# Sparse attention into a gated MLP: a new start-up, k copied out of PSUM, and a plan that prices tile-mode changes

## The chip, the cores and the metric

The kernel runs on one core of a Trainium2 chip. A core has TensorE (PE: matmuls; weight loads are listed apart as PEld), VectorE (DVE), ScalarE (ACT), GpSimd (POOL), a queue engine (SP), and DMA engines that move data between HBM and the on-chip memory SBUF. Matmuls write into a small second memory, PSUM. The metric is the time of one execution on the device in microseconds (us), the median of three runs.

## The reference, cut to what matters

```python
# q, k, v: (4, 8, 768, 64) float32; chunks of 32 keys, 24 chunks, top_k = 6
k_min, k_max = k_chunks.min(axis=3), k_chunks.max(axis=3)
ub = sum(maximum(q * k_min, q * k_max), axis=-1)      # bound of a query for a chunk
ub = where(causal, ub, -1e9)
top_chunks = argsort(ub)[..., -6:]
mask = chunk_is_selected & (pos_q >= pos_k)
attn = softmax(where(mask, q @ k.T / 8, -1e9)) @ v
x = attn, heads side by side                          # (3072, 512)
h = x @ w_in                                          # (512, 2048)
out = (h * clip(h + 3, 0, 6) / 6) @ w_out             # (2048, 512)
```

The first 192 queries have at most six chunks behind them, so the selection matters for the other 576 only.

## The kernel before

**Attention.** Two heads of one batch form a pair; there are 16 pairs, four per batch. A pair passes through these steps, named by the letters of the plan:

- k, q, v: loads of 384 KB each, as two DMA issues, one per head. The first pair's second halves of k and q go out on ScalarE's queue, everything else on SP's.
- K: six fp32 transposes on PE (tile KT, in PSUM); DVE reduces each 32 keys to maximum (KM) and minimum (KC) and subtracts; ScalarE casts KT to bf16 (LHS). All three read KT in PSUM.
- Q: six transposes (QT); ScalarE copies them to SBUF (QTS); DVE clips at zero (QP); GpSimd casts QTS to bf16 (RHS).
- U: 24 small matmuls, 64 rows by 32 columns of the array, give the chunk bounds (UBP); DVE adds the causal bias (UBT).
- V: four transposes (UBQ); twelve 8-maximum searches on DVE; a comparison with the sixth largest gives SEL.
- L: three transposes (SLT) and a copy (SELT).
- S: scores in six groups per pair (tile SPS, matmuls with 64 rows, two heads side by side in the array). To each group further matmuls of EM with SELT add a large negative number at chunks that were not selected. ScalarE takes the exponential (PT); GpSimd zeroes what lies above the diagonal.
- C: GpSimd casts v to bf16 (VB), with a column of ones.
- P: 21 matmuls per head (PVP); DVE divides by the sum and writes to the row block Xb.

**MLP.** Tokens go in eight groups of 384, two per batch. X transposes Xb (XTP), H multiplies by w_in (tile HP, 64 blocks of eight matmuls), ScalarE and DVE form the gated value GT, and O multiplies by w_out (tile OP, 24 output tiles, each of four blocks of four matmuls). ScalarE scales each output tile and SP stores it. The weights come in eight chunks (w0 to w3 for w_in, w4 to w7 for w_out), issued from GpSimd's queue and cast to bf16 on the way.

**What sets the order.** Nothing is looped in program order. All operations go into a list scheduler (class Plan) that knows a duration for each, their dependencies and the number of buffers per ring (for instance three large PSUM buffers, "big", shared by KT, QT, UBP, SPS and HP). For each engine it takes the operation that could start first; PE may choose, among those that could start within 0.1 us of each other, the one that stands earlier in a long written list of tokens (SEQUENCE). The instructions are then emitted in that order, so every engine works strictly through its own list and waits in place. Weight chunks are tied to the cast of a certain pair's v by WGATE.

On PE the operations use three tilings of the array: U uses 64 by 32, S uses 64 by 128, and the others a single tile.

Lines of the profile: KT and QT transposes L301, reductions L311, subtraction L319, LHS L326, QTS L337, QP L341, RHS L347, UBP L360, UBT L368, UBQ L382, SLT L410, SPS L440 and L445, exponential L451, diagonal L455, PVP L480, HP L537, OP L561, output copy L567, store L570. Constants are made once, ahead of the first operation (L230 to L253).

Of the kernel before, what the change touches and what calls it, by code (L numbers as in the profile page):

```python
# [15 lines left out]
P = 128  # L16
CH = 32
# [5 lines left out]
LAT = {"PE": 0.22, "DVE": 0.09, "ACT": 0.09, "POOL": 0.09, "LD": 2.0, "ST": 2.0}  # L23

# [6 lines left out]
class Op:  # L31
    def __init__(self, eng, dur, tok, key, fn, deps, take, use):
        self.eng, self.dur, self.tok, self.key, self.fn = eng, dur, tok, key, fn
        self.deps = [d for d in deps if d is not None]
        self.take = take
        self.end = None
        for t in list(take) + list(use):
            t.users.append(self)
        self.banks = [t for t in list(take) + list(use) if t.ring in ("big", "sm")]


class Plan:


    def __init__(self, rings, start, place):
        self.place = place
        self.rings = {r: [None] * n for r, n in rings.items()}
        self.count = {r: 0 for r in rings}
        self.free = dict(start)
        self.ops = []  # L50
        self.last = {}

    def add(self, eng, dur, tok, fn=None, deps=(), take=(), use=(), chain=None):
        deps = list(deps)
        if chain is not None:
            deps.append(self.last.get(chain))
        op = Op(eng, dur, tok, self.place(tok), fn, deps, take, use)
        if chain is not None:
            self.last[chain] = op
        self.ops.append(op)  # L60
        return op
# [18 lines left out]
    def run(self, slack):  # L80
# [9 lines left out]
        while any(cand.values()):  # L90
            best = None
            for eng, lst in cand.items():
                mine = None
                for op in lst:
# [3 lines left out]
                    at = max(r, self.free[eng])  # L98
                    s = slack.get(eng, 0.0)
# [9 lines left out]
            self.free[op.eng] = op.end  # L109
            for b in op.take:  # L110
                b.slot = self.count[b.ring] % len(self.rings[b.ring])
                self.rings[b.ring][b.slot] = b
                self.count[b.ring] += 1
# [8 lines left out]

SEQUENCE = """
V0 S0.2 R0 K0 k2 q1 R3 w7 q0 S0.4 S0.1 U0 k3 v5 v0 R1 P0.0 v6 w4 S3.0 R2 S0.0 v1 S0.3 S0.5 V2 V4 k0 w0 k4 w6 Q3
V3 K1 L2 q5 P0.1 v3 w5 S2.2 R7 k1 Q1 R6 k5 H1.8 O1.2.8 w3 K2 H1.6 S3.1 v10 L5 S3.5 L3 q3 S3.4 U2 K4 C5 K3 R4
S3.2 H1.10 v2 O1.2.4 S3.3 H1.4 Q8 X1.2 Q7 Q2 S1.3 P-1.0 K5 L0 P-1.1 R5 S2.5 w2 H2.0 S1.0 k7 S2.0 V11 S1.1 K6 V5
H1.2 q4 S11.1 O1.2.0 H0.10 H2.2 U1 q11 O3.2.8 C0 P2.0 H0.0 k6 R9 S1.5 S1.2 H2.4 H1.14 K8 H2.6 L7 S1.4 S4.4 H1.0
H0.8 U6 Q6 v8 k11 H2.12 V6 Q4 w1 H4.6 P1.0 k9 H2.10 S4.5 S2.1 L4 O1.1.12 S4.2 Q0 q8 S2.4 U3 v4 U9 H4.4 H0.6  # L130
H0.12 v11 O3.0.8 P7.0 S4.3 R10 S7.0 S2.3 P5.0 P3.0 S4.0 H4.12 U5 P4.1 O1.1.8 H2.14 S4.1 S5.4 P5.1 S5.1 H4.0 K10
P6.1 H1.12 U4 U8 X5.0 C4 L8 U7 k14 H4.2 R8 O1.2.12 q7 v7 H4.10 H0.2 Q5 v15 S5.3 q6 H6.10 S6.2 S5.0 X1.0 v9 H7.2
k12 H4.8 V7 C14 K9 O3.1.0 H0.4 C3 v12 O1.0.12 O1.1.4 S5.2 S5.5 S6.1 H2.8 P9.0 S6.3 S7.5 v13 S7.1 V10 H0.14 X6.0
q14 S6.5 P4.0 P6.0 H7.12 S6.4 R11 V1 V8 K7 O3.0.4 C2 k8 O1.1.0 X2.0 O3.2.0 C10 O3.2.12 S7.2 O1.0.0 v14 S10.2 C9
P1.1 P10.0 P11.0 O0.1.8 O1.0.4 P2.1 S6.0 P8.0 O0.2.8 Q9 L1 X7.2 U10 X0.0 P11.1 S9.0 H6.0 S9.4 L6 S7.4 S7.3 X4.0
H3.12 O3.0.0 P8.1 O3.1.8 q10 H7.4 q2 R15 S9.3 C1 P7.1 O0.2.4 V9 O0.1.12 H5.2 X0.2 P9.1 L12 O3.0.12 K11 H3.6 Q10
Q11 P3.1 H5.14 U13 S10.4 O1.0.8 H7.0 H6.12 S8.5 S8.0 O3.1.12 S8.2 O0.0.12 X5.2 O3.2.4 O0.0.4 S9.1 S10.1 S13.5
H6.4 U12 P10.1 O2.0.0 q9 V13 S13.1 L14 H6.6 S10.5 Q12 H6.14 L9 S8.3 C11 X3.2 P12.1 L11 H7.14 R12 O3.1.4 S8.4 C6
H4.14 P14.0 S9.2 S10.0 S10.3 X2.2 S12.2 U14 H5.4 X6.2 S11.4 S8.1 S13.0 X3.0 H3.8 P12.0 O0.1.0 U11 S9.5 S14.4 K12
S11.3 L10 O0.0.0 C12 R14 O4.0.8 O4.1.8 O2.0.8 k10 H3.10 O0.2.12 X7.0 C8 O4.0.0 k15 O2.0.4 H3.4 O4.1.0 S13.3 C13  # L140
L15 S13.2 O2.1.8 O2.1.4 H3.0 O2.0.12 C7 O0.1.4 V15 H7.6 K13 q13 H3.2 H6.8 O2.2.8 S11.2 S11.5 H5.10 O2.1.12 S14.1
K14 S12.4 S11.0 S14.0 O4.2.8 K16 H7.8 H5.8 q15 Q16 k13 H6.2 O4.2.0 H3.14 O0.0.8 H5.12 O4.2.12 K17 U15 S12.5
P13.1 O0.2.0 O4.1.12 Q15 K15 P14.1 Q17 O4.1.4 O4.0.4 U16 V16 O2.2.12 K18 O2.1.0 L16 Q14 Q18 S14.5 Q13 H7.10
S13.4 S12.1 q12 P15.1 U17 V17 H5.0 O4.2.4 K19 S12.0 S16.0 O2.2.4 S12.3 V12 L17 S15.1 S14.2 Q19 X4.2 S16.1 S16.2
U18 S16.3 L13 V18 S16.4 O2.2.0 V14 O5.1.0 S16.5 O4.0.12 H5.6 S15.3 C15 S14.3 P13.0 O5.0.0 S15.0 O5.2.12 P15.0
O6.0.12 O6.1.0 O5.2.4 O5.0.8 S15.2 S15.4 O5.1.4 O5.1.12 O7.0.8 O6.0.8 O6.0.0 O7.1.8 O5.2.8 O7.1.4 O6.0.4 S15.5
O6.2.12 O6.2.0 O6.2.4 O5.1.8 O7.0.12 O7.0.4 O6.2.8 R13 O7.2.0 O7.1.12 O6.1.4 O6.1.12 O6.1.8 O7.2.12 O7.2.4
O7.0.0 O7.2.8 O7.1.0 O5.2.0 O5.0.12 O5.0.4
# [4 lines left out]
def place(tok):  # L153
    return POS.get(tok, 0)
# [3 lines left out]
def kernel(  # L158
# [31 lines left out]
    rings = dict(big=3, sm=2, ks=3, qs=3, vb=3, vs=3, qts=3, qp=2, kc=4, lhs=4, rhs=4, ubt=2, sel=2, selt=3,  # L190
                 pt=9, x=4, xt=2, gt=2, u=3, ot=2)
    plan = Plan(rings, dict(PE=2.0, DVE=3.2, ACT=2.2, POOL=5.0, LD=0.3, ST=0.0), place)
# [23 lines left out]
    THREE = const.tile([P, 1], FP32, name="THREE")  # L216
    EM = const.tile([P, 2, S], BF16, name="EM")
# [13 lines left out]
    def constants():  # L231
        make_identity(nc, IDENT32[:])
        nc.vector.memset(THREE[:], 3.0)
        for t in fixed["kc"]:
            nc.vector.memset(t[:], 0.0)
# [16 lines left out]
        for g in range(4):  # L252
            nc.vector.tensor_copy(EM[g * CH:(g + 1) * CH, g % 2], E32[:])  # L253


    st = [dict() for _ in range(NP)]

    def plan_loads(i):
# [4 lines left out]
        def ld(buf, x, name):  # L263
            t = new(buf, [P, NBLK, 2, D], FP32, name)
            for e in range(2):
                (nc.scalar if i == 0 and e == 1 and x is not v else nc.sync).dma_start(
                    t[:, :, e, :], natural(x, b, 2 * hp + e))
# [4 lines left out]
        s["ldk"] = add("LD", 2.07, f"k{i}", lambda: ld(s["ks"], k, "KS"), take=[s["ks"]], chain="ldk")  # L272
        s["ldq"] = add("LD", 2.07, f"q{i}", lambda: ld(s["qs"], q, "QS"), take=[s["qs"]], chain="ldq")
        lv = add("LD", 2.07, f"v{i}", lambda: ld(s["vs"], v, "VS"), take=[s["vs"]], chain="ldv")
        s["o_v"] = add("POOL", 0.86, f"C{i}", castv, deps=[lv], take=[s["vb"]], use=[s["vs"]], chain="castv")

    WGATE = (2, 2, 3, 3, 4, 4, 5, 5)

    def plan_weights():
# [3 lines left out]
        for n in range(4):  # L283
# [4 lines left out]
            res.append(add("LD", 3.1, f"w{n}", None, deps=[iss], chain="w"))  # L288
        for n in range(4):
# [4 lines left out]
            res.append(add("LD", 3.1, f"w{n + 4}", None, deps=[iss], chain="w"))  # L294
# [8 lines left out]
    UDUR = 0.74  # L303

    def plan_K(i):
        s, tok = st[i], f"K{i}"
        kt = Buf("big")
        s["kc"], s["lhs"] = Buf("kc"), Buf("lhs")
        tr = add("PE", 0.66, tok, lambda: transposed(kt, s["ks"], "KT"), deps=[s["ldk"]], take=[kt], use=[s["ks"]], chain="K")
        def stat(op, dst):  # L310
            nc.vector.tensor_reduce(out=dst, in_=kt.obj[:, 0:S].rearrange("p (c w) -> p c w", w=CH), axis=AX.X, op=op)  # L311
# [5 lines left out]
        def sub():  # L317
            t = fx(s["kc"])
            nc.vector.tensor_tensor(out=t[:, 0, 0:NCH], in0=s["KM"][:], in1=t[:, 1, 0:NCH], op=A.subtract)  # L319
        a1 = add("DVE", 0.95, tok, smax, deps=[tr], use=[kt])  # L320
        a2 = add("DVE", 0.95, tok, lambda: stat(A.min, fx(s["kc"])[:, 1, 0:NCH]), deps=[tr, a1], take=[s["kc"]],
                 use=[kt], chain="kc")
        s["o_kc"] = add("DVE", 0.45, tok, sub, deps=[a2], use=[s["kc"]])

        def lhs():
            nc.scalar.copy(new(s["lhs"], [P, S], BF16, "LHS")[:], kt.obj[:, 0:S])  # L326
        s["o_lhs"] = add("ACT", 0.80, tok, lhs, deps=[a2] if i == 0 else [tr], take=[s["lhs"]], use=[kt], chain="lhs")

    def plan_Q(i):
# [13 lines left out]
        s["o_qp"] = add("DVE", 0.62, tok, part, deps=[up], take=[s["qp"]], use=[qts], chain="qp")  # L343
        s["qts"], s["o_qts"] = qts, up
# [5 lines left out]
    def plan_U(i):  # L350
# [13 lines left out]
        o = add("PE", UDUR, tok, mm, deps=[s["o_kc"], s["o_qp"], s["o_qts"]], take=[ub],  # L364
# [56 lines left out]
    def plan_S(i, m):  # L421
# [31 lines left out]
        def mask():  # L453
# [4 lines left out]
        o = add("PE", 0.09 + cols / 2400.0, tok, mm, deps=[s["o_lhs"], s["o_rhs"], s["o_slt"]], take=[sp],  # L458
                use=[s["lhs"], s["rhs"], s["selt"]])
        x = add("ACT", 1.03 if w > 256 else 0.40, tok, ex, deps=[o], take=[pt], use=[sp])  # L460
# [41 lines left out]
    def plan_mlp(g, wdma):  # L502
# [52 lines left out]
        def do_o(t, acc):  # L555
            ps, ot = Buf("sm"), Buf("ot")
# [15 lines left out]
            add("ST", 0.70, "", store, deps=[c], use=[ot], chain="store")  # L572

# [20 lines left out]
    small = ctx.enter_context(tc.tile_pool(name="small", bufs=4))  # L594
    for i in range(NP):
        plan_loads(i)
    wdma = plan_weights()
    for i in range(NP):
        for f in (plan_K, plan_Q, plan_U, plan_V, plan_L):
            f(i)  # L600
        for m in range(len(BINS)):
# [43 lines left out]
```

The softmax here doesn't subtract the row's maximum and nothing guards it: scores larger than these inputs give would overflow.

## Time and profile before

The median is 314.17 us (313.96 to 317.83 in three runs); the profiled execution spans 314.1 us.

| engine | busy us | share | instructions |
|---|---|---|---|
| PE | 292.0 | 93% | 2992 |
| PEld | 178.4 | 57% | 2992 |
| DVE | 173.8 | 55% | 464 |
| ACT | 178.6 | 57% | 217 |
| POOL | 78.1 | 25% | 149 |

| the program's parts on PE | matmuls | busy us |
|---|---|---|
| O (OP, L561) | 384 | 88.9 |
| H (HP, L537) | 512 | 85.9 |
| scores (SPS, L440 and L445) | 640 | 67.4 |
| k and q transposes (L301) | 192 | 29.8 |

Busy shares are means over stages with different limits: the first 60 us are attention alone, from then on attention of later pairs runs between the MLP's blocks, and the last 45 us are MLP alone. What counts for a change is therefore where in the span PE isn't busy, and at what clock it runs. A matmul's busy time can overlap the next one's, so the time of a block is better read from its start to the start of what follows it. DMA moves 29.82 MB, 24.78 MB of it through SP's and ScalarE's queue, most of it in the first third.

### The profile page before, as it was taken

To read this page: it belongs to the slowest core of one execution; us is meant where nothing else is said; L and a number is where in the kernel's file an instruction comes from. 1 tells how busy PE (TensorE), PEld (TensorE's weight loads), DVE (VectorE), ACT (ScalarE), POOL (GpSimd) and SP (SyncE) were. 2 spreads that over 40 slices of the span, in tenths; PEclk is the share of its full clock that TensorE was granted. 3 is DMA by queue.
4 is the path that set the end of the run, shared out by engine and by line. 5 is a ranking of instruction groups with operands and counts; after the bars stand their busy time and mean duration, and the time that the engine had idled before them with its cause. 6 is when DMAs were issued, how large, how long until landed. Compare 5 with 4: busy or idle time off the path is not lost.

```text
span 314.1 us, 7230 instructions
## 1 busy us (share of the span) xinstructions
PE 292.0 (93%) x2992; PEld 178.4 (57%) x2992; DVE 173.8 (55%) x464; ACT 178.6 (57%) x217; POOL 78.1 (25%) x149
## 2 busy tenths in 40 slices
PE   3569789889999999999999999999999999999995
PEld 2437557556665566466656566466646655665442
DVE  7358777757574854287656656157705612577100
ACT  0338878747857456176868554366464781566111
POOL 7137667411312032150343013130120221000000
PEclk9979999979999999999999999999999999999999
DMA  9994999996402575550232000100011000000121
GB/s 210 279 262 86 221 219 212 218 257 140 102 16 66 138 182 129 146 136 1 49 88 53 0 33 35 69 33 2 0 35 68 2 35 35 33 0 3 44 89 67
DMA packets 82976, 29.82 MB, mean 95 GB/s; under 512 B 75776, under 2 KB 79872, under 8 KB 82944
## 3 DMA queue, kind: packets, MB, share of 16 engines
q1 hardware_dynamic: 77152, 24.78, 32.1%
q0 software_dynamic: 4224, 4.19, 8.2%
q10 hardware_dynamic: 1568, 0.39, 0.6%
q8 instruction: 23, 0.38, 0.5%
q14 instruction: 9, 0.07, 0.1%
HBM read 27.26 MB, written 6.29 MB: 107 GB/s over the span
## 4 chain that ended last, share of the span: by engine, by line
PE 87%; DVE 5%; ACT 3%; DMA 2%; POOL 1%; issue 1%; SPq 0%; ACTq 0%; POOLq 0%
PE OP L561 27%; PE HP L537 26%; PE PVP L480 7%; PE SPS L440 7%; PE SPS L445 5%; PE UBP L360 4%; PE KT L301 3%; PE QT L301 3%; DMA QS<-in_q_dram 2%; PE UBQ L382 2%; PE XTP L517 2%; ACT PT L451 1%; DVE KM L311 1%; PE SLT L410 1%; DVE EM L253 1%
## 5 line engine op out<-in xcount | busy, mean ns | idle before, releaser
L451 ACT ACTIVATE PT<-SPS 128x1024 bf16<-128x1024 f32 (+1 forms) x96 | 83.1, 924 | 21.8 <-PE SPS L445 19.6
L561 PE MATMUL OP<-WOUT,GT 128*128 128x512 bf16 x384 | 88.9, 379 | 0.0
L537 PE MATMUL HP<-XT,WIN 128*128 128x384 bf16 x512 | 85.9, 326 | 0.0
L541 ACT ACTIVATE U<-HP,THREE 128x768 bf16<-128x768 f32 x64 | 57.7, 902 | 35.5 <-PE HP L537 35.5
L547 DVE SCALAR_TENSOR_TENSOR GT<-U,HP 128x768 bf16<-128x768 bf16 x64 | 61.0, 953 | 27.6 <-ACT U L541 27.6
L537 PEld LDWEIGHTS <-WIN 128*128 128x128 bf16 x512 | 49.5, 98 | 32.1 <-issue 0.7
L455 POOL TENSOR_SCALAR_AFFINE_SELECT PT<-PT 128x256 bf16<-128x256 bf16 x96 | 38.6, 408 | 111.5 <-ACT PT L451 111.2
L561 PEld LDWEIGHTS <-GT 128*128 128x128 bf16 x384 | 35.5, 98 | 40.6 <-issue 2.4
L567 ACT ACTIVATE OT<-OP 128x512 f32<-128x512 f32 x24 | 14.4, 600 | 51.6 <-PE OP L561 41.0
L440 PE MATMUL SPS<-RHS,LHS 64*128 64x512 bf16 (+3 forms) x256 | 35.0, 315 | 0.8 <-ACT PT L451 0.7
L445 PE MATMUL SPS<-SELT,EM 64*128 64x288 bf16 (+6 forms) x384 | 32.4, 252 | 0.0
L347 POOL CAST RHS<-QTS 128x768 bf16<-128x768 f32 x16 | 15.7, 984 | 40.7 <-ACT QTS L337 39.5
L480 PEld LDWEIGHTS <-PT 128*128 128x128 bf16 x672 | 23.4, 97 | 2.8 <-issue 1.0
L445 PEld LDWEIGHTS <-EM 64*128 64x128 bf16 x384 | 18.7, 96 | 7.9 <-issue 1.0
L311 DVE TENSOR_REDUCE KM<-KT 128x24 f32<-128x768 f32 x16 | 15.1, 956 | 11.9 <-PE KT L301 11.8
L440 PEld LDWEIGHTS <-LHS 64*128 64x128 bf16 x256 | 11.3, 95 | 14.0 <-issue 10.8
L301 PE MATMUL KT<-IDENT_111,KS 128*128 128x128 f32 x96 | 14.6, 296 | 4.6 <-DMA KS<-in_k_dram 4.2
L326 ACT CAST LHS<-KT 128x768 bf16<-128x768 f32 x16 | 12.8, 801 | 10.1 <-DVE KM L311 8.5
L490 DVE TENSOR_TENSOR Xb<-PVP,RINV 128x384 bf16<-128x384 f32 x32 | 17.7, 556 | 1.0
L301 PE MATMUL QT<-IDENT_111,QS 128*128 128x128 f32 x96 | 15.2, 304 | 2.6 <-DMA QS<-in_q_dram 2.2
L368 DVE TENSOR_TENSOR UBT<-UBP,BIAS 96x384 f32<-96x384 f32 x16 | 8.8, 551 | 15.1 <-PE UBP L360 15.0
L337 ACT COPY QTS<-QT 128x768 f32<-128x768 f32 x16 | 12.6, 804 | 5.6 <-PE QT L301 5.5
(103 smaller groups left out, 217.4 us busy)
## 6 DMA issues: line engine op xcount, KB each, us to landing
VS<-in_v_dram SPq DMA_DIRECT2D x32, 192.0 KB, 3.5
out_dram<-OT SPq DMA_DIRECT2D x24, 256.0 KB, 2.0
KS<-in_k_dram SPq DMA_DIRECT2D x31, 192.0 KB, 3.2
QS<-in_q_dram SPq DMA_DIRECT2D x31, 192.0 KB, 3.4
WIN<-in_moe_w_in_dram POOLq DMA_DIRECT2D x4, 512.0 KB, 9.2
WOUT<-in_moe_w_out_dram POOLq DMA_DIRECT2D x4, 512.0 KB, 8.4
KS<-in_k_dram ACTq DMA_DIRECT2D x1, 192.0 KB, 3.3
QS<-in_q_dram ACTq DMA_DIRECT2D x1, 192.0 KB, 4.3
```

Source lines behind the costliest of these rows:

```text
L301: nc.tensor.transpose(T[:, j * P:(j + 1) * P], src.obj[:, j].rearrange("p e d -> p (e d)"), IDENT32[:])
L311: nc.vector.tensor_reduce(out=dst, in_=kt.obj[:, 0:S].rearrange("p (c w) -> p c w", w=CH), axis=AX.X, op=op)
L440: nc.tensor.matmul(T[:, e, c:c + hi - lo], lhsT=s["lhs"].obj[e * D:(e + 1) * D, j * P:(j + 1) * P], rhs=s["rhs"].obj[e * D:(e + 1) * D, lo ...
L445: nc.tensor.matmul(T[:, e, c:c + hi - lo], lhsT=EM[e * D:(e + 1) * D, h, j * P:(j + 1) * P], rhs=s["selt"].obj[e * D:(e + 1) * D, x:x + hi ...
L451: nc.scalar.activation(T[:, :, 0:w], sp.obj[:, :, 0:w], ACT.Exp, scale=scale)
L455: nc.gpsimd.affine_select(out=dv, in_=dv, pattern=[[0, 2], [1, P]], compare_op=A.is_ge, fill=0.0, base=0, channel_multiplier=-1)
L480: nc.tensor.matmul(T[:, qb, :], lhsT=t[:, e, c:c + P], rhs=fx(s["vb"])[:, e, j, :], start=(j == 0), stop=(j == qb))
L490: nc.vector.tensor_tensor(out=xb[b].obj[:, :, h * D:(h + 1) * D], in0=pv.obj[:, :, 0:D], in1=s[("ri", e)][:].to_broadcast([P, NBLK, D]), o ...
L537: nc.tensor.matmul(T[:, f, 0:GRP], lhsT=WIN[:, kt, (f0 + f) * P:(f0 + f + 1) * P], rhs=xt.obj[:, kt, :], start=(kt == 0), stop=(kt == KT_H ...
L541: nc.scalar.activation(new(u, [P, 2, GRP], BF16, "U")[:], hp.obj[:, :, 0:GRP], ACT.Relu, bias=THREE[:], scale=1.0)
L547: nc.vector.scalar_tensor_tensor(out=gt.obj[:, f0:f0 + 2, :], in0=u.obj[:], scalar=6.0, in1=hp.obj[:, :, 0:GRP], op0=A.min, op1=A.mult)
L561: nc.tensor.matmul(T[:, :], lhsT=gt.obj[:, f, t * P:(t + 1) * P], rhs=WOUT[:, f, :], start=(f == 0), stop=(f == FT - 1))
```

## The change

It has five parts.

1. Start-up. A one-column exponential (WARM) right after the constant THREE makes ScalarE load its function table at once. Ten transposes of the identity ahead of the first k transposes, and nine behind the first q transposes, keep PE at work while it would wait (plan_warm); their results are not used. The four copies that fill EM move from DVE to GpSimd.
2. Loads. v is planned after the next pair's q, and the weights' gates change.
3. From pair 1 on, ScalarE copies the transposed k to SBUF as fp32 (KTS); the reductions and the cast to LHS, now on GpSimd, read that copy. Pair 0 stays as it was.
4. The plan counts a change of PE's tiling as 0.095 us (SWITCH) and asks that a pair's scores follow all of the pair before; some planned durations change, and SEQUENCE is a new list, so the order is new throughout.
5. The last output tile is computed, copied and stored in two halves of 256 columns (do_last).

```diff
-    def add(self, eng, dur, tok, fn=None, deps=(), take=(), use=(), chain=None):
+    def add(self, eng, dur, tok, fn=None, deps=(), take=(), use=(), chain=None, mode=0):
...
                     at = max(r, self.free[eng])
+                    if eng == "PE" and op.mode != self.mode:
+                        at += SWITCH
...
+        nc.scalar.activation(WARM[:], THREE[:], ACT.Exp, scale=-1.0)
...
         for g in range(4):
-            nc.vector.tensor_copy(EM[g * CH:(g + 1) * CH, g % 2], E32[:])
+            nc.gpsimd.tensor_copy(EM[g * CH:(g + 1) * CH, g % 2], E32[:])
...
+        s["ldv"] = add("LD", 2.07, f"v{i}", lambda: ld(i, s["vs"], v, "VS"), deps=[st[min(i + 1, NP - 1)]["ldq"]],
+                       take=[s["vs"]], chain="ldv")
...
-    WGATE = (2, 2, 3, 3, 4, 4, 5, 5)
+    WGATE = (0, 0, 0, 4, 4, 0, 8, 3)
...
+        direct = i == 0
+        if direct:
+            src, up = kt, tr
+        else:
+            def copy():
+                nc.scalar.copy(new(kts, [P, S], FP32, "KTS")[:], kt.obj[:, 0:S])
+            src, up = kts, add("ACT", 0.80, tok, copy, deps=[tr], take=[kts], use=[kt], chain="kts")
...
         def lhs():
-            nc.scalar.copy(new(s["lhs"], [P, S], BF16, "LHS")[:], kt.obj[:, 0:S])
+            (nc.scalar.copy if direct else nc.gpsimd.tensor_copy)(new(s["lhs"], [P, S], BF16, "LHS")[:], src.obj[:, 0:S])
...
-        o = add("PE", 0.09 + cols / 2400.0, tok, mm, deps=[s["o_lhs"], s["o_rhs"], s["o_slt"]], take=[sp],
+        o = add("PE", 0.02 + cols / 2400.0, tok, mm, mode=1, deps=[s["o_lhs"], s["o_rhs"], s["o_slt"]] + (st[i - 1]["S"] if i else []), take=[sp],
...
+    def plan_warm(n, after):
+        w = Buf("sm")
+
+        def mm():
+            T = new(w, [P, P], FP32, "WRM")
+            for _ in range(WARMUP[n]):
+                nc.tensor.transpose(T[:], IDENT32[:], IDENT32[:])
+        return add("PE", 0.2 * WARMUP[n], f"W{n}", mm, deps=[after], take=[w], chain="warm")
```

WARMUP is (10, 9). In do_last the only new operations are 32 matmuls of 128x256 in place of 16 of 128x512, and two copies and two stores of half the size.

## The prediction

> **What bounds the kernel now.** I read the slices first, then stage windows, then the timeline of the stages that are not full, and last the chain for prices. Slices of the page (each 7.85 us; tenths):
>
> ```profile
> PE   3569789889999999999999999999999999999995
> ...
> PEclk9979999979999999999999999999999999999999
> DMA  9994999996402575550232000100011000000121
> ```
>
> The reader should see that PE is full from about slice 9 to the last one, that the DMA engines are full in slices 0 to 8, and that the clock dips in slices 2 and 8. The stage windows (us; PE, PEld, DVE, ACT, POOL busy; clock; DMA share; GB/s):
>
> ```profile
> 4.15:22.00 17.85, 10.70 (x89) 7.53 (x91) 10.73 (x28) 4.39 (x5) 5.74 (x8) 0.94 1.24 280
> 22.00:60.40 38.40, 34.21 (x581) 25.04 (x578) 28.57 (x99) 32.23 (x39) 26.44 (x47) 0.99 1.05 187
> 60.40:67.30 6.90, 4.71 (x30) 3.16 (x28) 3.92 (x28) 1.70 (x2) 0.82 (x1) 0.77 1.14 252
> ...
> 80.00:310.60 230.60, 229.99 (x2171) 134.14 (x2167) 120.04 (x286) 129.77 (x161) 39.68 (x80) 1.00 0.20 57
> 310.60:314.10 3.50, 0.00 (x0) 0.00 (x0) 0.00 (x0) 0.59 (x1) 0.00 (x0) 0.88 0.20 75
> ```
>
> From 80 us on PE idles 0.6 of 230.6 us, so the end is PE's sum of work plus what PE lost before 67.3 us plus a 3.5 us tail. The timeline of the lossy stages:
>
> ```profile
> 4.15 1.51 PE L301 MATMUL KT<-IDENT_111,KS 128*128 128x128 f32 x6 [4.15 <-DMA KS<-in_k_dram]
> ...
> 8.12 1.28 ACT L326 ACT_TABLE_LOAD   x1 [8.12 <-DVE KC_122 L311]
> ...
> 17.66 1.04 DVE L341 TENSOR_SCALAR QP<-QTS 128x576 f32<-128x576 f32 x1
> ...
> 17.80 0.30 PE L410 MATMUL SLT<-IDENTB,SEL_126 96*128 96x96 bf16 x3 [1.43 <-DVE SEL_126 L393]
> ...
> 64.04 1.47 PE L301 MATMUL QT<-IDENT_111,QS 128*128 128x128 f32 x6 [2.19 <-DMA QS<-in_q_dram]
> ...
> 65.94 0.45 PE L410 MATMUL SLT<-IDENTB,SEL_127 96*128 96x96 bf16 x3
> ```
>
> Six transposes take 1.5 us cold against 0.66 later; a table load of 1.28 us stands in the first pair's chain; at 61.9 us PE waits 2.2 us for a q load and comes back cold. Prices from the chain of waits in order of time (start, us):
>
> ```profile
> 90.33 1.33 PE PVP L480 x42
> ...
> 99.31 1.97 PE KT L301 x18
> ...
> 104.73 0.80 PE UBP L360 x24
> ...
> 154.48 0.97 PE OP L561 x4
> ...
> 157.02 0.86 PE OP L561 x4
> ...
> 268.99 20.80 PE HP L537 x128
> 289.79 20.73 PE OP L561 x96
> ```
>
> Six k or q transposes are 0.655, a PVP head 0.67, an H group of eight 1.30, an O group of four 0.86; the same O group is 0.97 when a differently tiled matmul follows, so a change of tile mode costs 0.10. A UBP block ends in one such change, so it is 0.70 itself. From starts to starts in the full stretch also: UBQ 0.33, SLT 0.13, six XTP 0.34, the six score groups of a pair 2.27.
>
> **What the Trainium skill says.** (1) "TensorE: Matmul & The Clock Gate", Part 1: the clock is halved until one window of about 3.4 us has been busy, and falls back after an idle one. The trace agrees: its clock records are 3.41 us long, and the q transposes at 64.04 take 1.47 us. (2) The same page, Part 4, says that the clock doesn't engage for transposes. The trace disagrees: the SLT at 17.80 ran in 0.30 us, the warm length (0.45 at 65.94, cold), and the window before it (12.9 to 16.3) held mostly k, q and UBQ transposes. So transposes as clock keepers can work. A window 57% busy (2.7 to 6.1) did not warm the clock, however. (3) "TensorEngine Tiling (Array Packing)", Key Properties: changing the tiling mode drains TensorE; the 0.10 us above is that. (4) "GPSIMD Engine Reference", Specifications: its SBUF interface is shared with VectorE in two-port modes; QP took 1.04 us at 17.66 beside an RHS cast, 0.46 alone at 10.95.
>
> **The change, part by part.**
>
> Constants. The first ACTIVATE sits behind the loads instead of at 8.12, so the 1.28 us table load leaves the chain. The four EM copies (0.58 each) go from DVE to GpSimd: KM of pair 0 starts at 5.7, not 6.21. EM is needed only by the first score mask, after 15 us, so four GpSimd copies of 0.6 to 0.8 us, from 6.0 to about 9, cost nothing. The price: the second q half is issued on ScalarE's queue behind the table load, and may be issued 1.3 us later (issue at 1.33 before). Then q lands near 7 instead of 5.65. Hidden if the clock is warm, because the LHS copy of pair 0 precedes QTS on ScalarE and ends near 8.45 anyway.
>
> First chain: KT 4.15 to 5.66, KM and KC 5.7 to 7.6, LHS 7.6 to 8.45, QTS to 9.25, QP to 9.75, UBP at 9.8 (11.46 before). The warming transposes (10 from about 1.5 us at 0.25 cold, 9 after QT) make PE nearly continuous from 1.5 us on, so the clock should be full by then: UBP 0.80 instead of 1.52, ending 10.6 instead of 12.98. They lie in time when PE waits for loads. If the clock stays cold, the 9 (2.3 us) and the k transposes behind them (1.5 us) stand in front of UBP and it starts near 12.
>
> Then DVE in its new order: UBT 0.55, two reductions of pair 1 1.9, maxima 1.16, QP 0.46 to 1.04, subtraction 0.2 to 0.8, selection 0.45, two reductions of pair 2 1.9, SELT 0.3: 6.9 to 8.1, taken as 7.4. Mask matmuls follow, and the first exponential starts near 18.7 (22.0 before; 21.5 if cold).
>
> k copied to SBUF: ScalarE's 0.80 us copy replaces its 0.80 us cast, so ScalarE pays nothing; GpSimd gets 15 casts of 0.83 to 1.12 us (about 15 us), beside 78 busy of 314. In the attention stage this makes it 6 x 0.41 + 3 x 1.0 = 5.5 us a pair against ScalarE's 7.2: not the bound, though masks and DMA issues queue behind casts. The KT bank comes free after one 0.8 us copy, not after two reductions and a cast (2.7 us), which feeds the score groups better.
>
> Loads. v moves behind the next pair's q. Weight chunks, in before all eight issued between 26 and 54 us, stand in the built GpSimd order three after the first v cast (about 16 us), three after 26 score masks (about 51), two after 42 (about 73). Queue 0 took 8.2% of the span for eight, 3.2 us of all engines each. The jam of 30 to 64 us goes, and with it the 2.2 us wait for q and the cold stretch behind it: from 60.4 to 67.3 PE did 3.05 us of warm work, so 3.85 us come back. The last two chunks took 8.4 us to land before; needed near 89, they land by 85.
>
> Order of PE. Counting the built orders: mode changes 134 before, 116 after. Ahead of the first H group, before has 7 k and 7 q blocks, 7 UBP, 6 UBQ, 5 SLT, 29 score groups, 8 PVP, 2 XTP: 33.65 us, and 38 changes. After has 7, 7, 7, 7, 7, 38, 10, 4: 39.8 us, and 44 changes. So 6.15 us of work move ahead of the first H, and behind it 24 fewer changes (72 for 96) give 2.3 us.
>
> When does the first H start? Between the first exponential and H, ScalarE has 38 exponentials (32 of 1.03, 6 of 0.40) and 8 copies of 0.80: 41.9 us; PE has 38 us there. ScalarE becomes the bound of this stage. It was 94% busy in the densest ten microseconds before (50 to 60), 84% over 22 to 60.4. I take 94%: 18.7 + 44.6 = 63.3, less 2 us by which PE runs ahead through the three PSUM buffers: H at 61.3 (60.4 before).
>
> Tail. The last O tile is in two halves: the final copy is about 0.40 (the 128x256 exponential) for 0.60, the store half as large: 0.4 us.
>
> Sum: 314.1 + 0.9 - 6.15 - 2.3 - 3.85 - 0.4 = 302.3.
>
> **Rivals.** (A) As above, 302, chance 0.62; it needs ScalarE at 90% or more. (B) Better: a warm head and ScalarE at 100%, H at 58.6: 299.6, less 2 if the first exponential comes at 17: 298. For it: buffers and loads run well ahead. Against: ScalarE and PE are both near full and any slip shows. 0.18. (C) The new wait takes back most of it: the head stays cold (exponential at 21.5) and ScalarE stays at 84%: H at 21.5 + 49.9 - 2 = 69.4, end 310.4. For it: the late q half breaks PE's busy stretch, and a 57% window didn't warm. 0.15. (D) Slower: on top of C, GpSimd holds masks or the last weight chunks behind its casts, and O waits one landing of 8.4 us and returns cold (1.7): 320. Against: 16 us of slack, GpSimd at 75%. 0.05.
>
> **Numbers.** A is the likeliest: 302. B reaches down to 297; A and half of C reach up to 308.5, which leaves about 2 in 10 outside. 2% faster is 307.9: A, B and a little of C, 0.84; slower by 2% is part of D, 0.03; the rest 0.13.
>
> **What would show it.** Right: table load before 3 us; six k transposes of 0.66 us before 10 us; UBP near 9.8 and the first exponential near 18.7; no wait of QT for q near 60; ScalarE above 90% from 19 us to the first H near 61; PE full from there, with 72 mode changes. Wrong: the cold clock until 15 us or later, ScalarE waiting for score groups that wait for GpSimd's LHS or DVE's SELT, H after 65, or PE waits for weights between 70 and 90.

## The result, and the profile after

The changed kernel takes 306.13 us (median of four runs, 305.13 to 308.21) where the kernel before took 316.0 us on the same chip (313.96 to 317.98). The ratio is 0.970, with a 95% interval of 0.960 to 0.979: faster by 3%. The prediction was 302.0 us, range 297 to 308.5. The profiled executions span 304.2 us after and 314.1 us before. Medians below are over all runs of a kernel, ratios over the undisturbed ones only, so the two can differ by some tenths of a per cent.

The slices of the page (7.6 us each) answer to those shown of before:

```profile
PE   6977899999999999999999999999999999999995
...
PEclk9979999999999999999999999999999999999999
...
DMA  9999999995807989620200131100010000011012
```

The second dip of the clock, in slice 8 before, is gone, and PE is full from slice 5 on instead of slice 9. The first dip is still in slice 2. The DMA engines are as full as before in slices 0 to 8. The stage windows (us; PE, PEld, DVE, ACT, POOL busy with instruction counts; clock; DMA share; GB/s), cut where before's were:

```profile
4.15:22.00 17.85, 14.18 (x131) 10.91 (x133) 10.88 (x32) 6.66 (x9) 12.70 (x18) 0.90 1.38 217
22.00:60.40 38.40, 34.30 (x629) 25.02 (x627) 29.56 (x122) 32.00 (x39) 25.32 (x48) 1.00 1.07 203
60.40:67.30 6.90, 6.90 (x73) 4.32 (x68) 3.42 (x7) 6.20 (x8) 3.29 (x8) 1.00 1.19 195
```

From 60.4 to 67.3 us PE was busy for 4.71 of 6.90 us before, at clock 0.77; it is now busy for all of it at full clock. From 22 to 60.4 PE has 629 matmuls in the time that held 581. In the first row DMA moves 217 GB/s where it moved 280. The stage from the first exponential to the first H group, and from there to the last matmul, of the changed kernel:

```profile
19.94:63.55 43.61, 39.51 (x689) 28.41 (x686) 32.01 (x130) 37.19 (x45) 27.98 (x53) 0.98 1.09 203
63.55:300.70 237.15, 236.51 (x2224) 142.03 (x2221) 124.69 (x292) 134.91 (x166) 48.97 (x90) 1.00 0.30 71
```

Once H has begun, PE loses 0.6 us in 237 us. Before, the same stretch was 310.5 - 60.4 = 250.1 us. So 13.0 us came back behind the first H group, and 3.15 us of them were given up ahead of it (H at 63.55 for 60.4). That leaves 9.9 us, which is the difference of the two spans. The question for the experiments is why H began 3.15 us later and not 0.9. The timeline of the changed kernel's first 20 us has the start of it (start, busy us, engine, line, operation; in brackets the idle time before it and what ended that):

```profile
4.62 1.54 PE L319 MATMUL KT<-IDENT_114,KS 128*128 128x128 f32 x6 [0.80 <-DMA KS<-in_k_dram]
...
8.15 2.13 PE L650 MATMUL WRM<-IDENT_114 128*128 128x128 f32 x9
...
9.65 0.46 DVE L367 TENSOR_SCALAR QP<-QTS 128x576 f32<-128x576 f32 x1 [1.10 <-ACT QTS L363]
...
10.07 1.36 PE L319 MATMUL KT<-IDENT_114,KS 128*128 128x128 f32 x6
...
11.36 0.54 PE L386 MATMUL UBP<-QP,KC_126 64*32 64x192 f32 x12
...
17.36 0.30 PE L436 MATMUL SLT<-IDENTB,SEL_130 96*128 96x96 bf16 x3 [2.52 <-DVE SEL_130 L419]
...
17.64 1.63 POOL L302 DMA_DIRECT2D WIN<-in_moe_w_in_dram  x2
...
19.94 1.02 ACT L477 ACTIVATE PT<-SPS 128x1024 bf16<-128x1024 f32 x1 [4.21 <-PE SPS L471]
```

QP was done at 10.11, but UBP, which needs it, began at 11.36: the nine warming transposes and the six k transposes of pair 1, nearly all at half clock, stood in front of it in PE's list. At 17.64 two weight chunks are issued close together; a third goes out at 21.40. And this is PE's timeline from 18 to 75 us:

```profile
29.30 0.85 PE L319 MATMUL KT<-IDENT_114,KS 128*128 128x128 f32 x6 [2.14 <-DMA KS<-in_k_dram]
...
33.63 0.85 PE L319 MATMUL QT<-IDENT_114,QS 128*128 128x128 f32 x6 [0.73 <-DMA QS<-in_q_dram]
...
63.55 5.36 PE L564 MATMUL HP<-XT,WIN 128*128 128x384 bf16 x32
```

The wait for q near 62 us is gone; a wait of 2.14 us for k at 27 us and one of 0.73 us for q have come instead. The DMA queues of the changed kernel from 21 to 29 us (packets, MB, share of 16 engines; q0 carries the weights, q1 the loads of k, q and v):

```profile
q0 software_dynamic: 1317, 1.32, 97.5%
q1 hardware_dynamic: 1013, 0.26, 24.3%
```

Three chunks of 512 KB that are under way together take the engines almost for themselves. k, q and v get 0.26 MB through in 8 us; from 12 to 20 us, while no data of a chunk moved, it was 1.74 MB.

### The profile page after: what moved, and what is told of

Same layout as the page of the kernel before. It is cut to its first block, busy times and chain, and to the rows that moved or that the text cites. A ratio compares the mean times of both kernels' runs of the same rounds, so it can differ in the third digit from the quotient of the medians.

```text
span 304.2 us, 7326 instructions
## 1 busy us (share of the span) xinstructions
PE 290.5 (95%) x3027; PEld 182.0 (60%) x3027; DVE 168.8 (55%) x460; ACT 178.6 (59%) x219; POOL 92.0 (30%) x168
## 4 chain that ended last, share of the span: by engine, by line
PE 84%; DMA 6%; DVE 4%; ACT 2%; issue 1%; POOL 1%; SPq 1%; ACTq 0%; DVEq 0%; POOLq 0%
PE HP L564 27%; PE OP L590 26%; PE PVP L507 7%; DMA QS<-in_q_dram 6%; PE SPS L466 6%; PE SPS L471 4%; PE UBP L386 3%; PE QT L319 3%; PE KT L319 2%; PE XTP L544 2%; PE UBQ L408 2%; PE OP L611 1%; ACT PT L477 1%; DVE KM L337 1%; PE SLT L436 1%
## 5 line engine op out<-in xcount | busy, mean ns | idle before, releaser
L477 ACT ACTIVATE PT<-SPS 128x1024 bf16<-128x1024 f32 (+1 forms) x96 | 82.2, 924 | 18.1 <-PE SPS L471 15.7
L564 PE MATMUL HP<-XT,WIN 128*128 128x384 bf16 x512 | 86.8, 326 | 0.0
L590 PE MATMUL OP<-WOUT,GT 128*128 128x512 bf16 x368 | 84.1, 380 | 0.0
L466 PE MATMUL SPS<-RHS,LHS 64*128 64x512 bf16 (+3 forms) x256 | 34.1, 312 | 0.7 <-ACT PT L477 0.6
L512 DVE RECIPROCAL RINV<-PVP 128x6 f32<-128x6 f32 x32 | 6.0, 191 | 37.7 <-PE PVP L507 37.6
L352 POOL CAST LHS<-KTS 128x768 bf16<-128x768 f32 x15 | 12.4, 827 | 32.8 <-ACT KTS L333 30.0
L333 ACT COPY KTS<-KT 128x768 f32<-128x768 f32 x15 | 11.9, 800 | 9.5 <-PE KT L319 8.3
L319 PEld LDWEIGHTS KT<-IDENT_114,KS 128*128 128x128 f32 x96 | 11.8, 151 | 4.6 <-ACT PT L477 2.3
```

The lines of the kernel that those rows point to most:

```text
L319: nc.tensor.transpose(T[:, j * P:(j + 1) * P], src.obj[:, j].rearrange("p e d -> p (e d)"), IDENT32[:])
L466: nc.tensor.matmul(T[:, e, c:c + hi - lo], lhsT=s["lhs"].obj[e * D:(e + 1) * D, j * P:(j + 1) * P], rhs=s["rhs"].obj[e * D:(e + 1) * D, lo ...
L477: nc.scalar.activation(T[:, :, 0:w], sp.obj[:, :, 0:w], ACT.Exp, scale=scale)
L564: nc.tensor.matmul(T[:, f, 0:GRP], lhsT=WIN[:, kt, (f0 + f) * P:(f0 + f + 1) * P], rhs=xt.obj[:, kt, :], start=(kt == 0), stop=(kt == KT_H ...
L590: nc.tensor.matmul(T[:, :], lhsT=gt.obj[:, f, t * P:(t + 1) * P], rhs=WOUT[:, f, :], start=(f == 0), stop=(f == FT - 1))
```

## The experiments

They came in four groups, each with its own runs of the kernel before. In groups one to four those had medians of 315.55, 316.4, 316.78 and 316.25 us. Times of different groups are compared by their ratios to it. Four steps of the account are tested: the weights' place, the warming, the copy of k, and the start's other parts. "Full" and "half" clock are the two values in the profile's records of the granted clock; before a profile's first record the matmuls take the half-clock time.

### The two kernels again

The packets of k, q and v are 256 bytes each and took 18.0 ns from 4 to 20 us before, but 25.9 ns after. The first run asks whether that belongs to the chip.

> The kernel before, unchanged, profiled on the chip of the other runs of this group. Question: packets of 256 bytes took 18.0 ns each between 4 and 20 us in the kernel before and 25.9 ns in the changed one. Theory (the chip or the run decides): this profile shows one rate, and the changed kernel in the same group shows the same one. Rival (the change slows the loads, by its order of k and q without v or by GpSimd's longer use of SBUF): 18 ns here, near 26 in the changed kernel beside it. Time 314 to 318.

The kernel before, unchanged, took 314.69 us in one execution on the chip of group one, with packets of 17.9 ns.

> The changed kernel, unchanged, as the base for the kernels beside it. 0.97 of the kernel before (305 to 308). First exponential near 19.9, first H group near 63.5, a PE wait of some 2 us for a k load near 27 while the first three weight chunks land. [...]

The changed kernel, unchanged, on the same chip: 309.35 us (305.36 to 310.11), ratio 0.977 (0.972 to 0.982). This is the base for group one. Its packets took 25.8 ns, so the slower packets belong to the change, and the theory that they are the chip's falls. This is taken up again below.

The repeat's profile is of the slowest of its six executions (310.11 us, a span of 308.4), and it differs from the first one where it was expected to agree:

```profile
PEclk9979699999999999999999999999999999999999
...
31.98 1.51 PE L319 MATMUL KT<-IDENT,KS 128*128 128x128 f32 x6 [6.46 <-DMA KS<-in_k_dram]
```

Its head was quicker (clock full at 9.41 us, UBP at 10.40, first exponential at 18.40), but PE waited 6.46 us for k, the clock was at half from 29.89 to 36.71 us, and H began only at 67.72. From there to the last matmul it took 237.1 us, as in the first profile. So the same program in one execution began UBP at 11.36 and in another at 10.40, and lost 2 us or more than 6 to the wait for k. What one profile shows of either is partly chance.

### The weights apart

Theory: the three chunks issued together cost the wait for k, the slower clock behind it and the later H. Rival: loads are hidden, and something else in the stage sets H. Only the place of three issues in GpSimd's order is changed: each goes behind another v cast.

```diff
+ for tok, behind in (("w0", "C1"), ("w1", "C2"), ("w2", "C3")):
+     shift(tok, behind)      # GpSimd's list only; every other list as in the changed kernel
```

> The changed kernel with the first three weight chunks issued behind the casts of v of pairs 1, 2 and 3 (near 25, 37 and 46 us) instead of together behind pair 0's (18 to 21); every other order is the same. Theory (the three chunks together starve the k and q loads from 20 to 30 us and cost what the forecast missed): the 2.1 and 0.7 us waits for k and q at 27 and 33 go, the first H starts near 61.5 instead of 63.5, time 2 us less than the changed kernel beside it (0.964). Rival (ScalarE sets the pace of that stage anyway and takes up the wait): waits go, but H still starts near 63, under 0.7 us gained. Other rival: chunks that come later are late for H; PE waits between 64 and 75 and the time grows by 1 to 3 us.

It took 302.64 us (302.41 to 303.02), ratio 0.959 (0.955 to 0.963). Against the changed kernel's 0.977 on the same chip that is a further 0.9591 / 0.977 = 0.982, some 5.6 us. The intervals don't overlap. It is faster than both kernels, and the best of all that were run but for one equal to it. The slices of its page:

```profile
PEclk9999999999999999999999999999999999999999
```

There is no dip of the clock left. Its waits on PE for q and k (total us, times, longest):

```profile
PE QT L319 <- DMA QS<-in_q_dram: 1.2, 2, 0.7
PE KT L319 <- DMA KS<-in_k_dram: 1.2, 2, 0.8
```

The longest of each is in the head: 0.8 us for the first k, 0.7 for a q before 14 us. In the two profiles of the changed kernel, PE's waits for k are 2.9 and 7.3 us in all, of which 0.8 and 0.9 are for the first k. From 21 to 29 us the loads of k, q and v now move 1.06 MB, where they moved 0.26. The mean granted clock of the six executions is 0.992 to 1.000; in the six of the changed kernel beside them it was 0.981 to 0.989. The stage windows of the kernel with the weights apart, from its first exponential to its first H group and from there to near the end:

```profile
17.95:59.94 41.99, 39.18 (x689) 28.16 (x686) 32.24 (x130) 36.98 (x45) 29.89 (x55) 1.00 1.08 194
59.94:297.20 237.26, 236.62 (x2224) 142.03 (x2221) 124.05 (x292) 135.01 (x167) 49.20 (x90) 1.00 0.32 76
```

PE has the same 689 and 2224 matmuls in the two stages as in the changed kernel's first profile. Behind H nothing differs. Ahead of it the exponential comes 2.0 us sooner than in that profile and the stage is 1.6 us shorter; against the repeat, whose exponential came at 18.40, it is 0.45 us sooner and the stage 7.3 us shorter. No chunk is issued before 17 us, so what lies ahead of the exponential is not the chunks' doing. The timed runs carry the size of the gain, the profiles its place: the waits for k and the half clock behind them.

The same idea on the kernel before, where the eight chunks came between 26 and 54 us:

```diff
+ w1 behind C3, w2 behind C4, w3 behind C5, w4 behind C6, w5 and w6 behind C7, w7 behind C8
```

> The kernel before with the weight chunks issued one by one behind the v casts of pairs 2 to 8 instead of in pairs from pair 2 to pair 5 (26 to 54 us); all other orders as before. Theory (the weights' packets push the loads aside, and before paid that with the wait for q at 62 and the cold clock behind it): that wait and the cold stretch go, time 3 to 4 us less than before (0.988), spread between executions small. Rival (the loads of that stage are too many in any order): the wait stays or moves to another pair, gain below 1 us. Other rival: the last chunks are late for the first O groups near 95 us and the time grows.

It took 312.17 us (312.01 to 313.52), ratio 0.988 (0.984 to 0.991), and no wait for q is left near 62 us. The stage window:

```profile
60.00:80.00 20.00, 19.68 (x210) 13.48 (x199) 14.18 (x46) 14.58 (x17) 6.84 (x14) 1.00 0.67 132
```

From 60 us on PE is full at full clock. H began at 60.62 and the last matmul ended 246.3 us later, where the kernel before took 250.1. By the times, 316.4 x 0.0122 = 3.9 us, which is what the prediction gave for the wait and the cold stretch behind it. Part of the changed kernel's gain is thus to be had by moving issues alone.

### The warming

```diff
-            for _ in range(WARMUP[n]):
+            for _ in range(1):
```

> The changed kernel with one transpose instead of ten and one instead of nine in the two warming groups; all else the same. Theory (the second group and the cold k transposes behind it hold the first UBP until 11.4, but they buy a warm clock at 11.2): UBP starts near 9.9, runs cold (1.5 us), the following transposes are cold, the first exponential comes at 20.5 to 21, time 0.5 to 1 us more than the changed kernel. Rival (warming buys nothing, since DVE's chain of 7.4 us decides): first exponential at 19.9 or earlier, time the same or up to 1 us less.

With one transpose in place of ten and of nine: 309.21 us (306.18 to 310.5), ratio 0.979 (0.974 to 0.983), against 0.977 for the changed kernel. Its timeline shows UBP early but at half clock:

```profile
10.04 0.88 PE L386 MATMUL UBP<-QP,KC 64*32 64x192 f32 x12 [0.32 <-DVE QP L367]
```

UBP starts 1.3 us sooner than in the changed kernel's first profile and 0.4 sooner than in the repeat, because the nine transposes no longer stand in front. Its first exponential comes at 19.30, H at 64.35, and its wait for k near 29 us is 2.00 us, where the changed kernel's were 2.14 and 6.46. To take the chunks out of the picture, the same edit on top of the kernel with the weights apart:

> The changed kernel with the weights apart, and one transpose instead of ten and of nine in the two warming groups. Theory (warming pays by a clock that is full at 8 to 11 us): the clock is full only at 12 to 16 us, first exponential at 19 or later instead of 17.95, time 0.7 to 1.5 us more than with the weights apart alone. Rival (VectorE's chain decides; the clock of those 8 us costs nothing): within 0.4 us.

302.42 us (301.87 to 303.55), ratio 0.956 (0.952 to 0.960), beside 0.959 with the warming. First exponential 18.03 for 17.95, H 60.00 for 59.94, clock full at 9.75 for 8.42. The warming buys nothing that can be measured, with the jam or without it; a difference of under some 1.5 us would not show beside the intervals. The transposes of k and q bring the clock up by 9.75 us by themselves.

### The start's other parts

On the kernel with the weights apart, the EM copies go back to DVE:

```diff
-            nc.gpsimd.tensor_copy(EM[g * CH:(g + 1) * CH, g % 2], E32[:])
+            nc.vector.tensor_copy(EM[g * CH:(g + 1) * CH, g % 2], E32[:])
```

> The changed kernel with the weights apart, and the four EM copies back on VectorE. The start-up alone put the 256-byte packets from 18.0 to 25.9 ns for the first 20 us. Theory (the early table load or its exponential does that, since the packets slow down at 3 us and the EM copies on GpSimd run from 6 to 9): packets stay at 25.9 ns here; the first reduction waits for the copies, first exponential 0 to 0.6 us later, time within 0.7 us of the weights apart alone (302.6). Rival (GpSimd's use of SBUF slows the loads' writes): 18 ns, the first loads 0.5 us earlier, time 0.5 to 1 us less.

303.03 us (302.48 to 305.13), ratio 0.961 (0.955 to 0.968): 0.7 us later at the first exponential (18.64) and 0.8 at H (60.73) in the profile, within the intervals in the time. In that profile the clock was at half from 16.75 to 20.16 us, so the 0.7 us are not all the copies'.

Then the early table load is taken out, the copies staying on GpSimd:

```diff
-        nc.scalar.activation(WARM[:], THREE[:], ACT.Exp, scale=-1.0)
```

> The changed kernel with the weights apart and without the early exponential, so the table load of 1.28 us stands ahead of the first cast on ScalarE again, near 8 us; EM stays on GpSimd. Theory (the early table load slows the packets): 18.0 ns; the waits for k and q before 16 us shrink, the first chain gains 0.5 us by its load and loses 1.3 by the table, first exponential 18.5 to 19 (17.95), time 0 to 1 us more. Rival (EM on GpSimd slows them): 25.9 ns, first exponential 19.2, time 1 to 1.5 us more.

304.95 us (304.25 to 306.09), ratio 0.9675 (0.960 to 0.975). Its timeline:

```profile
8.21 1.28 ACT L351 ACT_TABLE_LOAD   x1 [8.21 <-DVE KC L336]
...
11.55 0.55 PE L385 MATMUL UBP<-QP,KC 64*32 64x192 f32 x12 [0.61 <-DVE QP L366]
```

The load is back in the first chain, UBP starts 1.3 us later than with the weights apart (10.21), and the first exponential (20.44) and H (62.42) come 2.5 us later. Here too the clock was at half for a while, from 17.23 to 20.64 us. By the medians of their own groups the early load is worth 302.64 to 304.95, 2.3 us, though the two ratios' intervals overlap.

Both parts alone on the kernel before:

```diff
+        nc.scalar.activation(WARM[:], THREE[:], ACT.Exp, scale=-1.0)
...
-            nc.vector.tensor_copy(EM[g * CH:(g + 1) * CH, g % 2], E32[:])
+            nc.gpsimd.tensor_copy(EM[g * CH:(g + 1) * CH, g % 2], E32[:])
```

> The kernel before with part of the start-up alone: the early one-column exponential and the four EM copies on GpSimd; no warming transposes, loads and order as before. Theory (the table load leaves the first chain, but the stage from 30 to 62 us is held by DMA): first UBP near 9.8 instead of 11.45, first exponential 1 to 1.6 us earlier (20.4), time at most 1 us less, the wait for q near 62 still there. Rival (the head counts in full): 1.5 to 2.5 us less. It shows also whether the 256-byte packets fall from 18.0 to 25.9 ns with this part of the change (then GpSimd or the early table load is behind it) or stay at 18.

321.17 us (318.1 to 323.44), ratio 1.012 (1.006 to 1.017): slower by about 1%, which neither theory had. The chain did get shorter (UBP 10.64 for 11.46, first exponential 21.18 for 22.0), but in its waits and on PE's timeline stands:

```profile
PE KT L303 <- DMA KS<-in_k_dram: 8.4, 2, 4.7
```

```profile
44.24 1.51 PE L303 MATMUL KT<-IDENT,KS 128*128 128x128 f32 x6 [3.65 <-DMA KS<-in_k_dram]
```

The longer of the two waits, 4.7 us, is that for the first k at the start (4.15 us before); the other is new. PE ran at half clock from 42.8 to 53.0 us, and H came at 66.50 instead of 60.4. The packets took 25.9 ns here too, and by 20 us the DMA engines had moved 3.97 MB where they had moved 5.01 MB before. An explanation that fits is that this kernel's loads are just in time, and with 1 MB less in SBUF there is no slack left when the chunks come. No run separates it from others, nor shows that the start pays only with the new order.

One more attempt at the head: the reductions of pair 2 behind the SELT copy of pair 0 in DVE's list, so that the first score masks come sooner.

```diff
- DVE: ... SEL(0), reductions(2), SELT(0) ...
+ DVE: ... SEL(0), SELT(0), reductions(2) ...
```

> The changed kernel with the weights apart, and on VectorE the two reductions of pair 2 put behind the SELT copy of pair 0, which the first score mask waits for; all else the same. Theory (VectorE's chain ahead of the first scores sets when ScalarE starts, and ScalarE sets the pace of the stage up to the first H): first exponential 1 to 1.3 us earlier (near 16.8), first H 0.5 to 1 us earlier, time 0.5 to 1 us less than the weights apart alone. Rival (what is gained is lost again where pair 2's bounds come later): within 0.3 us.

302.8 us (302.38 to 303.31), ratio 0.9595 (0.954 to 0.965): no gain. SELT began 1.1 us sooner (16.06 for 17.18), but in that profile the clock was at half from 16.05 to 19.47 us, and the first exponential came at 18.44 for 17.95. Whether the reordering is worthless or only met a slow clock stays open.

### The copy of k

Two kernels ask which of the copy's two possible benefits counts: the PSUM bank that comes free early, and the freedom to reduce later. Both start from the weights apart. In the first, k stays in PSUM: ScalarE casts LHS from there in the copy's place, and DVE must reduce right behind it; GpSimd's LHS casts go, and LHS and KC get a buffer for each pair.

```diff
             def copy():
-                nc.scalar.copy(new(kts, [P, S], FP32, "KTS")[:], kt.obj[:, 0:S])
+                kts.obj = kt.obj
+                nc.scalar.copy(new(s["lhs"], [P, S], BF16, "LHS")[:], kt.obj[:, 0:S])
+                smax(); stat(A.min, ...); sub()
...
```

> The changed kernel with the weights apart, and k not copied to SBUF: ScalarE casts the transposed k to bf16 out of PSUM in the place of the copy, VectorE reduces it out of PSUM right behind it, GpSimd's casts fall away; TensorE's order is the same. The large PSUM buffer is then held 2.7 us instead of 0.8 for each pair. Theory (the copy pays by freeing that buffer early): PE waits for a buffer behind 13 pairs, the first H starts at 62 to 63 instead of 59.9, time 2 to 4 us more than with the weights apart (302.6). Rival (three buffers are enough, or the saved GpSimd time makes up for it): within 1 us of it.

317.0 us (315.92 to 319.6), ratio 1.003 (1.001 to 1.006): all that the change had gained is lost, several times what was expected. The first exponential comes at 22.39 and H at 69.77. PE's longest waits:

```profile
PE SLT L442 <- DVE SEL L425: 4.9, 2, 3.4
PE UBQ L414 <- DVE UBT L400: 3.7, 3, 2.3
```

These are waits for DVE's selection steps. Waits that can be for a PSUM buffer are smaller: 1.4 us of KT for an LHS cast, 1.9 of QT for copies of QTS, 2.5 of scores for exponentials. So the second kernel keeps the copy to SBUF and GpSimd's cast, and only makes DVE reduce as early as the first one did (KC has a buffer for each pair here too):

```diff
             def copy():
                 nc.scalar.copy(new(kts, [P, S], FP32, "KTS")[:], kt.obj[:, 0:S])
+                smax(); stat(A.min, ...); sub()
...
```

> The changed kernel with the weights apart and k copied to SBUF as before, GpSimd casting it; only VectorE's reductions stand right behind the copy in its order, as they must when they read PSUM. It parts the 14.4 us that the kernel with k in PSUM lost to the one with the weights apart (317.0 against 302.6) into VectorE's order and the held buffer; first exponential 22.4 and first H 69.8 there, 17.95 and 59.9 with the weights apart. Theory (the held buffer is most of it): 304 to 308 us, first exponential near 19 to 21. Rival (the order that the copy makes free is most of it, since early reductions push the bounds and selections of earlier pairs back on VectorE): 311 to 317 us, first exponential near 22, first H near 67 or later.

318.57 us (316.4 to 321.32), ratio 1.011 (1.003 to 1.019), with H at 70.39: just as slow, though the bank is free after one copy. PE waits for the same two, 5.8 us for SEL and 4.6 us for UBT, and DVE's timeline shows why:

```profile
17.18 0.95 DVE L342 TENSOR_REDUCE KM<-KTS 128x24 f32<-128x768 f32 x1 [0.32 <-ACT KTS L335]
18.05 0.94 DVE L342 TENSOR_REDUCE KC<-KTS 128x24 f32<-128x768 f32 x1
...
19.91 0.44 DVE L424 TENSOR_TENSOR SEL<-UBQ,T 96x288 bf16<-96x288 f32 x1
```

SEL of the first pair, on which everything waits, comes at 19.91 behind two reductions of a later pair; with the weights apart alone it comes at 15.10. So in this order the early reductions alone cost the whole gain, and a bank that comes free early does not make up for it. That the bank's early release is worth nothing is not shown: the two kernels differ in GpSimd's casts as well, and none reduces late while it holds the bank. Neither order was planned anew for its case, so 317 us is the cost of the early reductions in this order, not the best that k in PSUM can give.

## Why the prediction was right, and where it was not

The direction and the main chain of reasons held: 302.0 forecast, 306.13 measured, inside the range. There is some luck in that: the repeat's median of 309.35 us, on another chip, lies just above the range's 308.5. By the prediction's steps, with the profile of 304.2 us:

- **From the first H on (right).** Forecast: 6.15 us of work moved ahead, 2.3 us for 24 fewer mode changes, 3.85 us of wait and cold clock, together 12.3. Measured: 250.1 to 237.15 us, 13.0. The wait's share is confirmed by itself (3.9 us, the weights apart on the kernel before). What is left, 246.3 to 237.15 or 9.1 us, stands beside 8.45 for the other two. The counts behind these are in the traces: up to the first H group PE changes its tiling 38 times before and 44 after, behind it 96 and 72 times; ahead of H the changed kernel has one UBQ block, two SLT blocks, 58 score matmuls, two PVP heads and two XTP blocks more, as forecast. The price of a change stands in the changed kernel's chain too, for an O group ahead of score matmuls with their other tiling, and one ahead of H with its own:

```profile
135.09 0.97 PE OP L590 x4
...
144.72 0.86 PE OP L590 x4
```

  Moved work and mode changes were not run apart, so their split rests on these counts and the 0.11 us between the two lines; 0.65 us is in neither.
- **"The jam of 30 to 64 us goes" (failed).** It moved to 21 to 36 us. The prediction counted the chunks' share over the whole span, 3.2 us of all engines each, and saw "three after the first v cast", but drew no load near them. Three such chunks are 9.6 us of all engines in one piece, in a stage where k, q and v had no slack. It cost a wait for k of 2.14 us in one profile and 6.46 in the other, and some 5.6 us of the time, as the weights apart showed. The repeat's H at 67.72 is near the 69.4 of rival C, but for this reason and not for C's cold head.
- **UBP at 9.8 (failed in the profile, as the case "near 12" that it had named; 10.40 in the repeat).** q's second half was issued at 1.41 and not late, but with the slower packets k and q landed later: KT began at 4.62 for 4.15, which took back what moving the EM copies had won, and QT at 6.85. QP was done at 10.11 where 9.75 was forecast. The rest is the clock, not full until 11.16: the nine warming transposes and the six of k, 3.5 us together, stood in front of UBP. The judgement that the warming would make PE "nearly continuous" was the wrong one. PE still waited 0.80 us for k and 0.68 for q, was busy for 72% of the clock's window from 4.33 to 7.75 us, and the clock stayed at half. The runs without the warming show that it buys nothing.
- **DVE's chain of 7.4 us (right in kind).** From UBP to the first exponential, where 8.9 was forecast (9.8 to 18.7), it took 8.6 us after (11.36 to 19.94), with a clock at half from 17.99 to 21.40, 8.0 in the repeat, and 7.7 us in the kernel with the weights apart (10.21 to 17.95). The Trainium skill ("TensorE: Matmul & The Clock Gate", Part 1) puts the fall of the clock down to an idle window; here the half clock follows a window, 14.57 to 17.99 us, in which PE waited 2.5 us for SEL and was busy for 26%. A window need not be wholly idle.
- **The QP reading (wrong in part).** The prediction has QP "alone" at 10.95 us. A cast of RHS ran from 10.97 to 12.09 us there too, so that line does not show what a cast costs QP: 0.46 us where the cast began just behind it, 1.04 where one was already under way.
- **ScalarE 94% busy up to H, PE 2 us ahead of it (wrong in size, the errors cancelling).** It was busy for 37.19 of 43.61 us, 85%, and 88% with the weights apart. But of the 41.9 us that the prediction counted for it, 4.7 were still to do when PE began H. So by that count PE ran 4.7 us ahead, not 2, and the stage took 43.6 us for 42.6. ScalarE is the most loaded engine beside PE there; that it bounds the stage is not shown.
- **"The KT bank comes free after one 0.8 us copy" (not what decides).** It does, but with early reductions the whole gain was lost all the same. What the prediction left out is that the copy lets DVE reduce later.
- **GpSimd is not the bound, EM on GpSimd is free (right).** No wait of weight on PE is put down to GpSimd's casts. The copies back on DVE changed the time by no more than the intervals.
- **Tail 0.4 us (mis-sized).** From the last matmul to the end it was 3.62 us before and 3.55 after. The final copy took 0.38 for 0.60, but from its end to the end of the span 3.1 us passed for 2.9: the half-size store did not end the program sooner.

With the two mis-sized terms replaced, the sum is 314.1 + 3.15 - 6.15 - 2.3 - 3.85 - 0.1 = 304.85, for a profile of 304.2; the difference is the 0.65 us behind H named above. The kernel with the weights apart is close to what the prediction had described: exponential at 17.95 (18.7), H at 59.94 (61.3), span 300.6 (302.3), 302.64 us timed (302.0). So the jam that stayed is worth about the difference between forecast and result.

The new order of the loads was not tested by itself, nor the new order of PE without the mode price.

## What to carry to other kernels

A large transfer costs its own time on all DMA engines at the moment of its issue: draw it against the loads that are due in that stretch, and space such transfers by the work that gives the others slack, rather than counting their share of the span. A copy out of PSUM can pay by letting an in-order engine do the reading later; test that apart from the buffer that it frees. Clock-keeping matmuls stand in the same queue as the work they are to speed up, and should be measured with and without. Profile the same kernel twice before a start time that differs by a microsecond is explained.

## What was not expected of the hardware

**Packet times.** From 4 to 20 us the 256-byte packets took 17.9 to 18.0 ns (274 GB/s in the stretch from 12 to 20 us) in the kernel before, in its repeat, and with its weights apart. They took 25.7 to 25.9 ns (218 GB/s) in every kernel that had part of the change's start-up, also without the early table load, with EM back on DVE, and without the warming. From 20 us on their means are 18 to 21 ns in all. Table load and EM copies together bring the slower packets on the old order; in the changed kernel neither is needed for them. Neither was run alone on the kernel before, so what causes them is open, and the changed kernel was faster in spite of them.

**Transposes and the clock.** In the changed kernel the window from 7.75 to 11.16 us held fp32 transposes only (QT, warming, KT), and the clock was full at its end. The same page of the Trainium skill says, in Part 4, that transposes don't bring up the clock; here, as in the kernel before, they did. The traces list them as MATMUL and don't show whether they ran in the transpose mode that the page means.

**How busy a window must be.** The records of the clock are 3.41 us long or multiples of it, so windows of that length can be laid back and forth from them, and the share of each in which the profile has PE busy can be worked out. In the fourteen profiles' first 90 us the clock went from half to full behind windows in which PE was busy for 84% or more, and stayed at half behind those with up to 80%; one window with 84% went each way. It fell behind windows with 0 to 51%, and held behind those with 49% or more, 49 to 51% going both ways. The windows lie differently in each execution: the changed kernel's head was full from 11.16 us in one and from 9.41 in the other.

**The table load.** In ScalarE's list the q issue stands behind the early load, and it went out at 1.41 us, while the load ran from 1.34 to 2.62: an issue of a transfer was not held up by it.
